# One weight conversion moved into the seam between two batches of attention, and the first query and key loads cut in two

## The chip, the cores and the metric

The kernel runs on one core of a Trainium2 chip. Its time is the device time of one execution in microseconds (us). Five engines work side by side, each through its own list of instructions in order: TensorE (PE, with its weight loads as PEld), VectorE (DVE), ScalarE (ACT), GpSimd (POOL), and SyncE (SP), which here only issues DMA transfers. They wait for each other through semaphores.

## The reference

Three stages follow one another. Sizes: 2 batches of 576 tokens, 8 heads of 64, width 512, inner width 1024, 8 experts.

```python
# windowed causal attention
scores = q @ k.T / sqrt(64);  rel = i - j
scores = where((rel >= 0) & (rel < 128), scores - slope[h] * abs(rel), -1e9)
attn = exp(scores - max(scores));  attn /= sum(attn) + 1e-9
x = (attn @ v) as (1152, 512)
# gated product
x = ((x @ w1) * (x @ w2)) @ w3 @ w_out
# one expert for each token, capacity 288 for each expert
probs = softmax(x @ w_gate);  e = argmax(x @ w_gate)
out[i] = probs[i, e] * (relu(x[i] @ E1[e]) @ E2[e])    # 0 where the expert is full
```

The weights w1, w2, w3 and w_out come as 64-bit floats.

## The kernel before

**Attention.** The work of a batch is cut into 4 pairs of heads, and a pair into 3 groups of query blocks (blocks 0 and 1, blocks 2 and 3, the last half block). So group k runs from 0 to 11 for batch 0 and from 12 to 23 for batch 1. For one group the steps are: `att_qk` (TensorE: scores, L233), `att_max` (DVE: add the bias, take the row extreme, L248), `att_exp` (ACT, L259), `att_norm` (DVE, L277, L278; in batch 1 also the scaling of the probabilities, L287), `att_tr` (TensorE transposes, L301, and copies out of PSUM, L303), `att_pv` (TensorE, L321). When a pair of batch 0 is complete, `att_fin` makes its output x: ACT copies the factors (L349), DVE multiplies (L351), and then x is split into a high part (ACT, L71) and a low part (DVE or POOL, L72).

**Conversions.** A piece of w1 or w2 (128x512 values of 64 bit, staged in one of 4 buffers by a 512 KB DMA, L123) becomes two fp32r tiles wh and wl, high and low part. `convert` gives three steps: `begin` (ACT, L135), `bits` (three DVE operations, L138 to L140), `parts` (wh by ACT at L71, then wl by POOL at L72, then the next DMA of the staging plan). The pieces are w_c_m_kp: column chunk c (0 to 3), matrix m (w1 or w2), half kp of the inner axis. The first four (chunk 0) are converted in groups 2, 5, 8 and 10. The other twelve go by the table `CONVS`, which says how many of them group 12 + i takes.

**Gated product of batch 0 between the groups.** In groups 12 to 23 `fill` puts halves of this product (`ab_half`, twelve matmuls of 288 columns, L376 to L378) between the attention steps, one or two at a time. A half with f = 2 or 3 reads chunk 1 of the weights, one with f = 4 or 5 reads chunk 2. ACT copies the w1 half out of PSUM (asb, L383), DVE multiplies the w2 half with it (g, L388). Two PSUM banks serve the halves in turn.

**The seam.** Group 12 is written out by hand: x of the last pair of batch 0 is finished while TensorE runs the part of two halves that doesn't need it (`part=0`), then the scores of group 13, three zero products (`warm_b`) and the rest of the first half.

**The start.** `keep_clock(12, "warm0")` issues twelve products of zeros (L81) on TensorE; `load_qk(0, 0)` and `load_qk(0, 1)` load the first two pairs: q, k and two pieces of v each. The scores of groups 0, 1 and 2 follow the zero products on TensorE.

The order of the work is the order of the code: the scheduler is off (`manual_schedule`), so each engine runs its instructions as they are written.

```python
CONVS = (0, 1, 1, 2, 1, 1, 2, 1, 1, 1, 1, 0)
        cvts = [c for c in (conv_next() for _ in range(CONVS[k - NGB])) if c]
        for c in cvts: c[0]()
        if k > NGB: fill(ab0, 1); att_tr(k - 1)
        if NGB < k < 2 * NGB - 1: att_qk(k + 1)
        for c in cvts: c[1]()
        if k > NGB: fill(ab0, 2 if k % 3 == 2 else 1)
        for c in cvts: c[2]()
        if k > NGB: att_pv(k - 1)
```

Of the kernel before, what the change touches and what calls it, by code (L numbers as in the profile page):

```python
# [18 lines left out]
P = 128  # L19
# [1 line left out]
BIGS = 31  # L21
STAGES = 4
WARM = (4, 4, 4, 2, 2, 2, 2, 2, 2, 2, 2)
CONVS = (0, 1, 1, 2, 1, 1, 2, 1, 1, 1, 1, 0)
OOB = 1 << 20


# [1 line left out]
def block_kernel(ctx: ExitStack, tc: tile.TileContext, qT, kT, v, w1, w2, w3T, wo, wg, e1, e2, out):  # L29
    nc = tc.nc  # L30
    B, H, D, S = qT.shape
# [26 lines left out]
    def slot(name, shape, dtype=F32R):  # L58
        t = big.tile([P, SLOT], dtype, tag="u", name=name)
        n = 1  # L60
        for d in shape:
            n *= d
        if len(shape) == 1:
            return t[:, :n]
        return t[:, :n].rearrange("p (a b) -> p a b", b=shape[1])

    def ps(tag, name):
        return psum.tile([P, 512], F32, tag=tag, name=name, bufs=2)
# [8 lines left out]
    def keep_clock(n, name):  # L77

        w = ps("t", name)
        for _ in range(n):  # L80
            nc.tensor.matmul(w, hot[:, :P], hot, start=True, stop=True)  # L81

    keep_clock(12, "warm0")


    WC = 256
# [73 lines left out]
    def load_qk(b, hp):  # L160
        h0 = 2 * hp
        t = slot(f"qk_{b}_{hp}", (2, S), F32)
        for i, src in enumerate((qT, kT)):
            nc.sync.dma_start(out=t[:, i, :], in_=src[b, h0 : h0 + 2].rearrange("h d s -> (h d) s"))
        vt = apool.tile([P, 6, P], F32, tag="v", name=f"v_{b}_{hp}", bufs=3)
        cs = slice(h0 * D, (h0 + 2) * D)
        nc.sync.dma_start(out=vt[:, 0:4, :], in_=v[b, 0 : 4 * P, cs].rearrange("(c p) d -> p c d", p=P))
        nc.sync.dma_start(out=vt[:TK, 4:6, :], in_=v[b, S - 2 * TK : S, cs].rearrange("(c p) d -> p c d", p=TK))
        qk[b, hp] = t, vt

    load_qk(0, 0)
    load_qk(0, 1)

    iota = cv.tile([P, 512], F32, tag="cvt", name="iota", bufs=3)[:, : 2 * P]
# [33 lines left out]
    def conv_w(c, m, kp):  # L208
        if kp == 0:
            wsb[m, c] = slot(f"wh{m}_{c}", (KD, WC)), slot(f"wl{m}_{c}", (KD, WC))  # L210
        return convert(("w", c, m, kp), *(w[:, 2 * kp : 2 * kp + 2, :].rearrange("p k f -> p (k f)") for w in wsb[m, c]), pool_hi=(c == 0))
# [12 lines left out]
    def att_qk(k):  # L224
        b, hp, g = groups[k]
        t = qk[b, hp][0]
        tag = "acc" if k <= NGB and k % 2 else "s"
        sps = [ps(tag, f"s{j}_{k}").rearrange("p (i w) -> p i w", i=2) for j in range(2)]
        for gj, i in enumerate(g):
            q0, M, k0, W, _, _ = blocks[i]  # L230
            for j in range(2):
                js = slice(j * D, (j + 1) * D)
                nc.tensor.matmul(sps[j][:M, gj, :W], t[js, 0, q0 : q0 + M], t[js, 1, k0 : k0 + W], start=True, stop=True)  # L233
        live["s", k] = sps

    def att_max(k, gj):
        b, hp, g = groups[k]
        if gj == 0:
            live["p", k] = [], apool.tile([P, 12], F32, tag="sm", name=f"stat_{k}", bufs=8)
        pp, st = live["p", k]  # L240
        i = g[gj]
        q0, M, k0, W, _, _ = blocks[i]
        off = P - (q0 - k0)
        p = apool.tile([P, 2, 2 * P], F32, tag="p", name=f"p_{k}_{i}", bufs=6)
        pp.append(p)
        for j in range(2):
            c = 2 * gj + j
            nc.vector.tensor_tensor_reduce(out=p[:M, j, :W], in0=live["s", k][j][:M, gj, :W],  # L248
                                           in1=relb[:M, 2 * hp + j, off : off + W], scale=-1.0 / isq, scalar=3.0e38,
                                           op0=ALU.add, op1=ALU.min, accum_out=st[:M, c : c + 1])  # L250

    def att_exp(k, gj):
        b, hp, g = groups[k]
        pp, st = live["p", k]
        p = pp[gj]
        _, M, _, W, _, _ = blocks[g[gj]]
        for j in range(2):
            c = 2 * gj + j
            nc.scalar.activation(out=p[:M, j, :W], in_=p[:M, j, :W], func=AF.Exp, scale=-1.0,  # L259
                                 bias=st[:M, c : c + 1], accum_out=st[:M, 4 + c : 5 + c])  # L260
# [97 lines left out]
    def att_fin():  # L358
        if fins:
            fins.pop(0)()  # L360
# [290 lines left out]
    def conv_next():  # L651
        return conv_w(*wq.pop(0)) if wq else None
# [10 lines left out]
    for k in range(NGB):  # L663
        b, hp, g = groups[k]
        if g[0] == 4:
            load_qk(*divmod(hp + 2, NPAIR))
        cvt = conv_next() if k in (2, 5, 8, 10) else None
# [30 lines left out]
    def fill(q, n):  # L698
        for _ in range(n):
            if q:  # L700
                u = q.pop(0)
                ab_half(*u, part=1 if u in begun else None)

    for k in range(NGB, 2 * NGB):
        b, hp, g = groups[k]
        if g[0] == 2 and hp + 2 < NPAIR:
            load_qk(1, hp + 2)
        if k == NGB:

            att_fin()  # L710
            att_norm(k - 1)
            att_tr(k - 1)
            att_pv(k - 2)
            att_pv(k - 1)

            for u in ab0[:2]:
                ab_half(*u, part=0)
            begun = ab0[:2]
            att_max(k, 0)
            att_exp(k, 0)  # L720
            att_fin()
            att_max(k, 1)
            att_exp(k, 1)
            att_fin()
            att_qk(k + 1)
            keep_clock(3, "warm_b")
            fill(ab0, 1)
        elif k == NGB + 1:
            att_soft(k, lambda: (att_norm(k - 1), fill(ab0, 1)))
            att_fin()  # L730
        else:
            att_soft(k, lambda: att_norm(k - 1))
            att_fin()
        cvts = [c for c in (conv_next() for _ in range(CONVS[k - NGB])) if c]
        for c in cvts:
            c[0]()
        if k > NGB:
            fill(ab0, 1)
            att_tr(k - 1)
        if NGB < k < 2 * NGB - 1:  # L740
            att_qk(k + 1)
        for c in cvts:
            c[1]()
        if k > NGB:
            fill(ab0, 2 if k % 3 == 2 else 1)
        for c in cvts:
            c[2]()
        if k > NGB:
            att_pv(k - 1)
# [34 lines left out]
    for i, u in enumerate(ab1):  # L784
# [3 lines left out]
        if i == 2:  # L788
            nc.sync.dma_start(out=disp[0 : E * CAP, :].rearrange("(p r) c -> p r c", p=P),
                              in_=zrow.unsqueeze(1).to_broadcast([P, E * CAP // P, RW]))  # L790
    for at in sorted(jobs):
        for job in jobs[at]:
            job()
    nc.sync.dma_start(out=out.rearrange("(p r) c -> p r c", p=P),
                      in_=zrow[:, :DM].unsqueeze(1).to_broadcast([P, NT // P, DM]))
# [86 lines left out]
    with (tc.If(fullest > N0), tc.tile_pool(name="over", bufs=2) as op,  # L882
          tc.tile_pool(name="overp", bufs=2, space=bass.MemoryType.PSUM) as opp):
        for e in range(E):
# [6 lines left out]
            for r in range(N0, CAP, P):  # L891
                n = min(P, CAP - r)
# [15 lines left out]
                for f in range(EF // P):  # L908
# [4 lines left out]
                    out=out, out_offset=bass.IndirectOffsetOnAxis(ap=x[:n, DM + 1 : DM + 2].bitcast(U32), axis=0),  # L913
                    in_=y[:n], in_offset=None, bounds_check=NT - 1, oob_is_err=False)
# [45 lines left out]
```

## Time and profile before

| what | value |
|---|---|
| time, median of 3 runs | 470.45 us (469.55 to 470.5) |
| the profiled execution: its own time | 469.5 us |
| the profiled execution: span from first to last instruction | 467.8 us |
| TensorE busy | 453.2 us, 97% of the span |
| VectorE, ScalarE, GpSimd busy | 68%, 56%, 31% |
| mean granted TensorE clock | 0.990 of full speed |

The profile is of one execution. 1.7 us of its own time lie outside the span. Matmuls are pipelined and overlap in the records, so a busy TensorE isn't one at its peak; a row in brackets tells how long the engine sat idle before an instruction and what ended the wait. Times in the rows are us from the start of the span. Rows of the timeline that are alike and stand together are merged, with their count behind an x.

### The profile page before, as it was taken

How to read it: one execution, taken by the hardware profiler on the slowest of the kernel's cores; microseconds unless marked ns; L12 is line 12 of the kernel's file. 1: busy time of each engine (PE TensorE's matmuls, PEld its weight loads, DVE VectorE, ACT ScalarE, POOL GpSimd, SP SyncE). 2: the span in 40 equal slices, each digit the busy share in tenths (PEclk: the TensorE clock that was granted, in tenths of full speed). 3: DMA queues.
4: the chain of work that ended last, by engine and by line, in shares of the span. 5: the costliest groups of instructions: out<-in, count | busy, mean ns of one | idle time of the engine just before them, and what ended most of it. 6: DMA issues, size and time to landing. Idle time of an engine off the chain costs nothing.

```text
span 467.8 us, 9288 instructions
## 1 busy us (share of the span) xinstructions
PE 453.2 (97%) x3346; PEld 405.2 (87%) x3346; DVE 320.0 (68%) x860; ACT 261.5 (56%) x653; POOL 144.9 (31%) x154
## 2 busy tenths in 40 slices
PE   8999999989999999999999999989999999999993
PEld 4667887869899999999999999689889898898982
DVE  6786768786542454788756777447888787888840
ACT  5786656465432345434444554246767677676740
POOL 2125113222111132344321111214365454544531
PEclk9999998989999999999999999999999999999998
DMA  8755325322159444585422434284786887868001
GB/s 273 242 183 184 100 74 189 98 84 90 47 170 245 130 136 130 186 303 163 145 89 69 136 136 137 87 296 162 235 291 205 303 243 238 282 206 284 27 1 54
DMA packets 30769, 77.77 MB, mean 166 GB/s; under 512 B 3582, under 2 KB 9214, under 8 KB 30720
## 3 DMA queue, kind: packets, MB, share of 16 engines
q1 hardware_dynamic: 28976, 72.41, 49.6%
q0 software_dynamic: 1744, 4.73, 2.7%
q8 instruction: 28, 0.46, 0.4%
q14 instruction: 21, 0.17, 0.1%
HBM read 65.30 MB, written 12.61 MB: 167 GB/s over the span
## 4 chain that ended last, share of the span: by engine, by line
PE 78%; DVE 10%; issue 6%; ACT 3%; POOL 2%; DVEq 0%; POOLq 0%; ACTq 0%
PE h L581 10%; PE ab L376 7%; PE ab L378 7%; PE ab L377 6%; PE h L582 5%; PE x L474 4%; PE x L475 4%; PE x L476 4%; DVE t_w L140 3%; PE s L233 3%; PE t L301 3%; PE oa L321 3%; PE y L612 3%; PE warm L81 3%; PE y L615 3%
## 5 line engine op out<-in xcount | busy, mean ns | idle before, releaser
L72 DVE TENSOR_TENSOR le<-st_e,he 128x1024 fp32r<-128x1024 f32 x64 | 78.3, 1225 | 28.4 <-ACT he L71 25.1
L376 PE MATMUL ab<-x,wh 128*128 128x288 f32 x256 | 80.3, 314 | 0.8 <-ACT wh L71 0.7
L378 PE MATMUL ab<-x,wl 128*128 128x288 f32 x256 | 76.4, 298 | 1.3 <-POOL wl L72 1.3
L581 PE MATMUL h<-xs,he 128*128 128x384 f32 x256 | 76.6, 357 | 1.1 <-DVE xs L72 1.1
L598 POOL CAST hs<-hs 128x64 fp32r<-128x64 f32 x64 | 53.7, 846 | 76.6 <-ACT hs L594 75.3
L377 PE MATMUL ab<-x,wh 128*128 128x288 f32 x256 | 75.8, 296 | 0.0
L71 ACT CAST he<-st_e 128x1024 fp32r<-128x1024 f32 x64 | 67.2, 1052 | 0.0
L582 PE MATMUL h<-xs,le 128*128 128x192 f32 x256 | 64.1, 251 | 0.0
L376 PEld LDWEIGHTS ab<-x,wh 128*128 128x128 f32 x256 | 48.6, 190 | 6.5 <-issue 2.4
L581 PEld LDWEIGHTS h<-xs,he 128*128 128x128 f32 x256 | 48.0, 188 | 3.8 <-DVE xs L72 1.2
L582 PEld LDWEIGHTS h<-xs,le 128*128 128x128 f32 x256 | 48.7, 190 | 1.9
L378 PEld LDWEIGHTS ab<-x,wl 128*128 128x128 f32 x256 | 48.6, 190 | 2.0 <-POOL wl L72 2.0
L377 PEld LDWEIGHTS ab<-x,wh 128*128 128x128 f32 x256 | 48.7, 190 | 0.0
L388 DVE TENSOR_TENSOR g<-ab,asb 128x288 f32<-128x288 f32 x32 | 14.6, 456 | 48.0 <-PE ab L378 45.8
L259 ACT ACTIVATE p<-p,stat 128x256 f32<-128x256 f32 (+2 forms) x80 | 37.3, 470 | 13.1 <-DVE stat L248 13.1
L588 ACT COPY cr<-h 128x192 f32<-128x192 f32 x64 | 20.5, 320 | 40.2 <-PE h L582 38.3
L474 PE MATMUL x<-wph,gh 128*128 128x260 f32 x144 | 41.4, 287 | 0.0
L476 PE MATMUL x<-wph,gl 128*128 128x260 f32 x144 | 40.6, 282 | 0.0
L475 PE MATMUL x<-wpl,gh 128*128 128x260 f32 x144 | 40.6, 282 | 0.0
L383 ACT COPY asb<-ab 128x288 f32<-128x288 f32 x32 | 12.7, 398 | 47.9 <-PE ab L378 47.9
L440 PE MATMUL wp<-woh,w3h 128*128 128x260 f32 x128 | 36.3, 283 | 0.5 <-DVE wpl L72 0.5
L442 PE MATMUL wp<-woh,w3l 128*128 128x260 f32 x128 | 36.2, 283 | 0.0
(139 smaller groups left out, 1075.1 us busy)
## 6 DMA issues: line engine op xcount, KB each, us to landing
st_e<-e SPq DMA_DIRECT2D x64, 512.0 KB, 4.4
st_w<-w SPq DMA_DIRECT2D x16, 512.0 KB, 4.4
st_w<-w3T SPq DMA_DIRECT2D x16, 512.0 KB, 4.2
disp<-zrow SPq DMA_DIRECT2D x1, 4626.0 KB, 21.3
st_wo<-wo SPq DMA_DIRECT2D x8, 512.0 KB, 3.8
qk<-qT SPq DMA_DIRECT2D x8, 288.0 KB, 4.8
qk<-kT SPq DMA_DIRECT2D x8, 288.0 KB, 5.1
y<-zrow SPq DMA_DIRECT2D x1, 2304.0 KB, 10.7
```

The source lines that it names most:

```text
L71: nc.scalar.copy(out=hi, in_=t)
L72: eng.tensor_tensor(out=lo, in0=t, in1=hi.bitcast(F32), op=ALU.subtract)
L259: nc.scalar.activation(out=p[:M, j, :W], in_=p[:M, j, :W], func=AF.Exp, scale=-1.0, bias=st[:M, c : c + 1], accum_out=st[:M, 4 + c : 5 + c])
L376: nc.tensor.matmul(a[:, :NCH], hi[:, fs], xh[:, n], start=first, stop=False)
L377: nc.tensor.matmul(a[:, :NCH], hi[:, fs], xl[:, n], start=False, stop=False)
L378: nc.tensor.matmul(a[:, :NCH], lo[:, fs], xh[:, n], start=False, stop=last)
L474: nc.tensor.matmul(pa[:, :HG], gh[:, kt, :], th, start=(kt == 0), stop=False)
L475: nc.tensor.matmul(pa[:, :HG], gh[:, kt, :], tl, start=False, stop=False)
L476: nc.tensor.matmul(pa[:, :HG], gl[:, kt, :], th, start=False, stop=(kt == KF - 1))
L581: nc.tensor.matmul(hp_[:, : 2 * N0], hi[:, kt, fs], xs, start=(kt == 0), stop=False)
L582: nc.tensor.matmul(hp_[:, N0 : 2 * N0], lo[:, kt, fs], xs[:, :N0], start=False, stop=(kt == KD - 1))
L598: nc.gpsimd.tensor_copy(h[:, 2 * N0 :], h[:, P:N0])
```

## The change

Three edits.

1. `CONVS` gives group 14 two conversions instead of one, group 15 one instead of two, and group 18 one instead of two. The group of the seam (12) keeps its 0 in the table, but its code now takes one conversion itself: `begin` ahead of the first maxima, `bits` ahead of the first `att_fin` there, `parts` behind the third. So the same sixteen conversions run in the same sequence; those of groups 13 to 17 and the first of group 18, seven in all, now stand one group earlier each (that of group 13 in the seam), and the second of group 18 and all later ones stand where they stood.
2. The zero products at the start are eight instead of twelve.
3. The first load of q and k is done in two column parts: columns 0 to 255 of q, the same of k, then columns 256 to 575 of each. It is four DMAs instead of two ahead of the first v.

```diff
-CONVS = (0, 1, 1, 2, 1, 1, 2, 1, 1, 1, 1, 0)
+CONVS = (0, 1, 2, 1, 1, 1, 1, 1, 1, 1, 1, 0)
-    keep_clock(12, "warm0")
+    keep_clock(8, "warm0")
 def load_qk(b, hp):
-        for i, src in enumerate((qT, kT)):
-            nc.sync.dma_start(out=t[:, i, :], in_=src[b, h0 : h0 + 2].rearrange("h d s -> (h d) s"))
+        for n in (slice(0, 2 * P), slice(2 * P, S)) if b == hp == 0 else (slice(0, S),):
+            for i, src in enumerate((qT, kT)):
+                nc.sync.dma_start(out=t[:, i, n], in_=src[b, h0 : h0 + 2].rearrange("h d s -> (h d) s")[:, n])
...
             begun = ab0[:2]
+            cvt = conv_next()
+            cvt[0]()
             att_max(k, 0)
             att_exp(k, 0)
+            cvt[1]()
             att_fin()
             att_max(k, 1)
             att_exp(k, 1)
             att_fin()
+            cvt[2]()
             att_qk(k + 1)
```

On DVE at the seam, before (x_w and t_w are tiles of a conversion, named w_c_m_kp; rs_3 is the product that makes x of pair 3; a number at a name's end only numbers the tile):

```order
L248 ISA p_12_0_762,stat_12_761<-s0_12_636,relb_117 128x128
L248 ISA stat_12_761 128x1
L248 ISA p_12_0_762,stat_12_761<-s1_12_637,relb_117 128x128
L248 ISA stat_12_761 128x1
L351 TENSOR_TENSOR rs_3_740<-oa_0_3_697,rs_3_740 128x512
L351 TENSOR_TENSOR rs_3_740<-ob_0_265,rs_3_740 128x64
```

and now:

```order
L250 ISA p_12_0_765,stat_12_764<-s0_12_634,relb_115 128x128
L250 ISA stat_12_764 128x1
L250 ISA p_12_0_765,stat_12_764<-s1_12_635,relb_115 128x128
L250 ISA stat_12_764 128x1
L138 TENSOR_SCALAR x_w_1_0_0_762<-st_w_1_0_0_434 128x512
L139 SCALAR_TENSOR_TENSOR x_w_1_0_0_762<-st_w_1_0_0_434,x_w_1_0_0_762 128x512
L140 SCALAR_TENSOR_TENSOR t_w_1_0_0_761<-t_w_1_0_0_761,x_w_1_0_0_762 128x512
L353 TENSOR_TENSOR rs_3_738<-oa_0_3_695,rs_3_738 128x512
L353 TENSOR_TENSOR rs_3_738<-ob_0_263,rs_3_738 128x64
```

The three steps of piece 1_0_0 now stand between the maxima and the product rs_3; on ACT its `begin` stands ahead of the exponentials of group 12 and its wh behind the high part of x.

On DVE at the end of group 15, before (g is the product of two halves, p_16 the maxima of the next group, stat_15 the norm of group 15):

```order
L388 TENSOR_TENSOR g_0_0_814<-ab1_0_1_1_1003,asb_0_1_1_966 128x288
L138 TENSOR_SCALAR x_w_1_1_0_998<-st_w_1_1_0_678 128x512
L139 SCALAR_TENSOR_TENSOR x_w_1_1_0_998<-st_w_1_1_0_678,x_w_1_1_0_998 128x512
L140 SCALAR_TENSOR_TENSOR t_w_1_1_0_997<-t_w_1_1_0_997,x_w_1_1_0_998 128x512
L138 TENSOR_SCALAR x_w_1_1_1_1000<-st_w_1_1_1_876 128x512
L139 SCALAR_TENSOR_TENSOR x_w_1_1_1_1000<-st_w_1_1_1_876,x_w_1_1_1_1000 128x512
L140 SCALAR_TENSOR_TENSOR t_w_1_1_1_999<-t_w_1_1_1_999,x_w_1_1_1_1000 128x512
L248 ISA p_16_2_1073,stat_16_1072<-s0_16_1024,relb_117 128x256
```

and now:

```order
L390 TENSOR_TENSOR g_0_0_824<-ab1_0_1_1_1020,asb_0_1_1_982 128x288
L138 TENSOR_SCALAR x_w_2_0_0_1018<-st_w_2_0_0_884 128x512
L139 SCALAR_TENSOR_TENSOR x_w_2_0_0_1018<-st_w_2_0_0_884,x_w_2_0_0_1018 128x512
L140 SCALAR_TENSOR_TENSOR t_w_2_0_0_1017<-t_w_2_0_0_1017,x_w_2_0_0_1018 128x512
L250 ISA p_16_2_1083,stat_16_1082<-s0_16_1041,relb_115 128x256
```

Both pieces of w2's chunk 1 have left this place for group 14, and the first piece of chunk 2 has come here.

On DVE at the end of group 18, before:

```order
L138 TENSOR_SCALAR x_w_2_1_0_1267<-st_w_2_1_0_1057 128x512
L139 SCALAR_TENSOR_TENSOR x_w_2_1_0_1267<-st_w_2_1_0_1057,x_w_2_1_0_1267 128x512
L140 SCALAR_TENSOR_TENSOR t_w_2_1_0_1266<-t_w_2_1_0_1266,x_w_2_1_0_1267 128x512
L138 TENSOR_SCALAR x_w_2_1_1_1269<-st_w_2_1_1_1147 128x512
L139 SCALAR_TENSOR_TENSOR x_w_2_1_1_1269<-st_w_2_1_1_1147,x_w_2_1_1_1269 128x512
L140 SCALAR_TENSOR_TENSOR t_w_2_1_1_1268<-t_w_2_1_1_1268,x_w_2_1_1_1269 128x512
L388 TENSOR_TENSOR g_0_1_1109<-ab1_0_3_1_1306,asb_0_3_1_1285 128x288
```

and now:

```order
L250 ISA stat_18_1259 128x1
L138 TENSOR_SCALAR x_w_2_1_1_1275<-st_w_2_1_1_1067 128x512
L139 SCALAR_TENSOR_TENSOR x_w_2_1_1_1275<-st_w_2_1_1_1067,x_w_2_1_1_1275 128x512
L140 SCALAR_TENSOR_TENSOR t_w_2_1_1_1274<-t_w_2_1_1_1274,x_w_2_1_1_1275 128x512
L390 TENSOR_TENSOR g_0_1_1117<-ab1_0_3_1_1308,asb_0_3_1_1290 128x288
```

Piece 2_1_0 has left group 18 for group 17. TensorE's own order is unchanged but for the four zero products; on SP, the load of piece 1_1_1 now stands ahead of the loads of q, k and v of batch 1's third pair, and the load of piece 2_1_1 ahead of those of its fourth.

## Rows read from the trace of the kernel before

**Rows 1.** The page's busy line: us (share of the span) xinstructions

```profile
PE 453.2 (97%) x3346; PEld 405.2 (87%) x3346; DVE 320.0 (68%) x860; ACT 261.5 (56%) x653; POOL 144.9 (31%) x154
```

**Rows 2.** PE's waits over the whole span: us in total, times, longest

```profile
PE t L301 <- DVE p L287: 2.0, 1, 2.0
PE ab L378 <- POOL wl L72: 1.3, 3, 0.8
```

**Rows 3.** Timeline of PE around group 15's product: start, us, what

```profile
69.09 0.46 PE L321 MATMUL ob<-pt,v 96*64 96x64 f32 x8
70.22 0.40 PE L376 MATMUL ab<-x,wh 128*128 128x288 f32 x1 [0.67 <-ACT wh L71]
...
71.58 0.40 PE L378 MATMUL ab<-x,wl 128*128 128x288 f32 x1 [0.83 <-POOL wl L72]
...
76.09 0.40 PE L376 MATMUL ab<-x,wh 128*128 128x288 f32 x1
```

**Rows 4.** Timeline of PE around group 18's transposes

```profile
91.56 0.46 PE L321 MATMUL ob<-pt,v 96*64 96x64 f32 x8
91.95 0.40 PE L376 MATMUL ab<-x,wh 128*128 128x288 f32 x1
...
95.78 1.41 PE L301 MATMUL t<-ident,p 128*128 128x128 f32 x6 [1.99 <-DVE p L287]
...
100.57 0.93 PE L321 MATMUL oa<-pt,v 128*64 128x128 f32 x12
```

**Rows 5.** Windows: us, busy PE PEld DVE ACT POOL, PEclk, DMA share, GB/s

```profile
73.00:73.50 0.50, 0.50 (x3) 0.50 (x4) 0.50 (x3) 0.00 (x0) 0.00 (x0) 0.50 1.32 381
97.00:98.00 1.00, 1.00 (x6) 0.34 (x5) 1.00 (x5) 1.00 (x5) 0.00 (x0) 0.50 0.00 0
```

**Rows 6.** Timeline of PE in groups 13 and 14: the same steps undisturbed

```profile
52.43 0.81 PE L301 MATMUL t<-ident,p 128*128 128x128 f32 x6
53.65 0.40 PE L376 MATMUL ab<-x,wh 128*128 128x288 f32 x1
...
55.44 0.93 PE L321 MATMUL oa<-pt,v 128*64 128x128 f32 x12
```

**Rows 7.** Timeline of the start: zero products, first scores, first conversion

```profile
1.25 4.22 PE L81 MATMUL warm<-hot 128*128 128x512 bf16 x12 [1.25 <-DVE hot L75]
...
4.21 0.77 PEld L81 LDWEIGHTS <-hot 128*128 128x128 bf16 x4 [0.28 <-issue]
...
5.41 2.75 PE L233 MATMUL s<-qk 64*128 64x128 f32 x20
...
11.58 0.68 ACT L135 ACTIVATE t_w<-st_w 128x512 f32<-128x512 f32 x1
```

**Rows 8.** DMAs issued at 1.0 to 1.5 and 4.6 to 5.0: us to landing

```profile
qk<-kT SPq DMA_DIRECT2D x1, 288.0 KB, 3.3
...
st_w<-w SPq DMA_DIRECT2D x1, 512.0 KB, 6.3
```

**Rows 9.** Timeline of the seam: the waits of DVE and ACT, POOL's work

```profile
42.63 1.41 POOL L72 TENSOR_TENSOR x<-rs,x 128x576 fp32r<-128x576 f32 x1 [0.16 <-ACT x L71]
...
45.28 0.59 ACT L349 COPY rs<-ra 128x512 f32<-128x512 f32 x1 [1.04 <-PE ra L344]
...
45.90 0.69 DVE L351 TENSOR_TENSOR rs<-oa,rs 128x512 f32<-128x512 f32 x1 [2.71 <-ACT rs L349]
...
50.27 0.40 ACT L383 COPY asb<-ab 128x288 f32<-128x288 f32 x1 [1.52 <-PE ab L378]
```

**Rows 10.** Lines L138 and L140 on DVE: duration ns min/median/max

```profile
L138 DVE TENSOR_SCALAR x_w<-st_w x32: 411/419/1461, 13.4 to 233.3; 128x512 int32<-128x512 int32 x32
L140 DVE SCALAR_TENSOR_TENSOR t_w<-t_w,x_w x32: 691/693/1625, 14.6 to 234.6; 128x512 int32<-128x512 int32 x32
```

**Rows 11.** Timeline around 70: POOL's two low parts, DVE's scaling

```profile
70.25 2.53 POOL L72 TENSOR_TENSOR wl<-t_w,wh 128x512 fp32r<-128x512 f32 x2 [4.62 <-ACT wh L71]
...
71.81 1.78 DVE L287 TENSOR_SCALAR p<-p,stat 128x128 f32<-128x128 f32 x4
```

## The prediction

> **What bounds the kernel now.** I read the page's busy line first. TensorE is busy 97% of the span and no other engine over 68% [rows 1], so time is to be had where TensorE stands still or runs slowly, and anything done on VectorE, ScalarE or GpSimd is free as long as TensorE doesn't wait for it. The second view is the list of TensorE's waits over the whole span. It is short, and two of its entries point at the conversions: 2.0 us once at a transpose that waits for VectorE's scaling of the probabilities, and 1.3 us in three waits for a low part of the weights from GpSimd [rows 2]. The third view is TensorE's timeline at these places.
>
> The first place is the w2 half of the product with f = 2, the first reader of w2's chunk 1. TensorE is done with `att_pv` of group 14 and waits 0.67 for the high part of piece 1_1_0, then 0.83 for its low part [rows 3]. Both pieces of that chunk are converted in group 15, just ahead of the reader. The second place is the transposes of group 18: the scaling comes 1.99 us late [rows 4], because two conversions stand ahead of it on VectorE.
>
> The fourth view, the windows, shows what a wait costs beyond itself. Behind both places the granted clock is 0.50 [rows 5], the lower of its two levels (1.2 GHz instead of 2.4), and the same instructions take about twice as long. TensorE had stood still for most of 2 us before each fall.
>
> **The first place.** From the start of `att_pv` to the second next product, TensorE takes 76.09 - 69.09 = 7.00 [rows 3]. The same steps undisturbed: `att_pv` of the half block 91.95 - 91.56 = 0.39 [rows 4], twelve products 55.44 - 53.65 = 1.79, transposes and scores 53.65 - 52.43 = 1.22 [rows 6], together 3.40. The wait and the slow clock behind it cost 3.60.
>
> The change converts these two pieces in group 14. Their reader then comes a whole group later, which is several us, while GpSimd's two low parts take 2.53 [rows 11]. So both waits go.
>
> **The second place.** From the twelve products to the next `att_pv` it is 100.57 - 91.95 = 8.62 [rows 4]. Undisturbed it is 1.79 + 1.22 + 1.79 = 4.80 [rows 6]. That costs 3.82. Of the two conversions of group 18 one moves to group 17. One conversion takes 0.42 + 0.69 + 0.69 = 1.80 on VectorE (L139 is like L140) [rows 10], almost all of the 1.99; and one of the two low parts leaves as well.
>
> What is late next? VectorE and GpSimd hold each other up. While GpSimd made two low parts, four scalings on VectorE took 1.78 [rows 11]; L138 takes 0.42 as a rule but up to 1.46, and L140 0.69 but up to 1.63 [rows 10]. So a scaling that meets a low part is up to about a GpSimd operation late. Half of the 2.53 for two is 1.27 for one. With the conversions one group earlier, the low parts fall at other moments of the groups, and the scaling ahead of the transposes of groups 13, 15 and 16 can meet one. I can't read from a trace of the old order how they fall. Each such meeting costs TensorE between nothing and 1.27. I take half, 0.6, at three places: +1.8 (ends 0 and +3.8).
>
> **The seam.** One conversion is added to group 12. VectorE idles for 2.71 ahead of the product of the last pair, from 43.19 to 45.90 [rows 9]. GpSimd's low part of x runs from 42.63 to 44.04 [rows 9], so L138, which can be held up by it, is taken to wait for its end. Then 44.04 + 1.80 = 45.84: just in time. Behind it are queued the product that makes x and two maxima, and TensorE waits for that x. There is 0.06 left, so I put +0.1 (ends: 0, and 1.8 if nothing is hidden).
>
> ScalarE gets `begin` (0.68 for the like instruction [rows 7]) ahead of the exponentials; it idles for 1.04 before the copy of the factors [rows 9]. The high part of the weight goes behind that of x and ahead of the copy of the first half, where it idles for 1.52 [rows 9]. Both are hidden, and the cover stays since TensorE sets the times of both copies.
>
> On SP the load of piece 1_1_1 now stands ahead of those of batch 1's third pair. The pair is needed four groups later, so I put nothing (to lose would be a wait of TensorE at its scores, which the trace doesn't show today).
>
> Group 14 now has two conversions, 3.60 on VectorE, ahead of a product of two halves that frees a PSUM bank. Group 15 had the same load before, in the same place of its code, and the waits there were for the weights, not for a bank [rows 3]. I put it into the +1.8.
>
> **The start.** Four zero products go. Their weight loads are (0.77 - 0.15)/3 = 0.21 apart [rows 7], the last 0.15 being one load's length, so four are 0.84. The first scores start at 5.41, when the products end at 1.25 + 4.22 = 5.47 [rows 7]. k has landed by 4.3 to 4.8 (issued between 1.0 and 1.5, 3.3 to land) [rows 8]. So today the products decide, and with eight, the scores could start at about 4.57, near the time at which a whole k lands. The first column parts are less than half the bytes and are all that group 0 reads, so the cut takes the loads out of the way there.
>
> Not all of the 0.84 will last. The first conversion's `begin` on ScalarE is at 11.58 [rows 7], and its weights land between 10.9 and 11.3 (issued between 4.6 and 5.0, 6.3 to land) [rows 8]. Moved up by 0.84 it would be at 10.74 and wait 0.2 to 0.6, with the copies of the transposes queued behind it on ScalarE. I take -0.6 for the start. Ends: -0.84; and, if a transfer of half the size took as long as a whole one, the loads behind would be late by up to the 3.3 of one [rows 8], so 3.3 - 0.84 = +2.5. The bytes are the same, so I stay near the first.
>
> The Trainium skill (DMA: Bandwidth & Descriptors, section on measured bandwidth) speaks against the cut: a small transfer reaches a smaller share of the rate, 0.95 us for 64 KB and 6.15 us for 1 MB. Drawing a line between the two, as an estimate, two parts of 128 KB and two of 160 KB take 5.5 us one behind the other, where two of 288 KB take 4.3; by that all later loads are 1.2 late and the sum is 0.8 to 1.2 smaller. No row here shows a 128 KB load by itself.
>
> **The sum.** -3.60 - 3.82 + 1.8 + 0.1 - 0.6 = -6.1. The profiled execution's own time is 469.5 (span 467.8 and 1.7 around it), so it becomes 463.4. The median of the runs is 470.45, 0.95 above the profiled execution. The forecast for the median is 470.45 - 6.1 = 464.3. Behind group 19 the order is unchanged, and no entry of TensorE's waits names a DMA [rows 2], so the gain should reach the end.
>
> **Rivals.**
>
> *The loads come late.* The mechanism is the one above: the four parts push the queue back and ScalarE's first conversion waits. For it: its weights have only 0.3 to 0.7 to spare. Against it: the same bytes. The start then gives about +0.3 instead of -0.6: 465.2.
>
> *One fall of the clock stays.* The meetings of scaling and low part add up to near 2 us at one place, as before both falls, and TensorE falls to the low clock again. For it: the 1.78 and the maxima of 1.46 and 1.63 [rows 10, 11]. Against it: fewer conversions at one place. One of the two gains goes, about 3.7, while the others hold: 468.0.
>
> *VectorE becomes the bound of groups 12 to 17: slower.* Seven conversions move one group earlier. If their 1.80 on VectorE lands on the way to a transpose or to x, each costs TensorE its full length. The gains without any new wait are 3.60 + 3.82 + 0.84 = 8.26, so it decides from 8.26/1.80 = 4.6, that is from five of seven. With six, 10.8 - 8.3 = +2.5: 473.0. For it: in the seam just 0.06 is left, and a late x delays everything. Against it: VectorE is busy 68% only [rows 1], and the same work was hidden one group later at all but two places.
>
> *Nothing comes of it.* A later stage takes the time back, as it waits for transfers: 470.5. Against it: no such wait in [rows 2].
>
> *All goes well.* No new wait: 470.45 - 8.26 = 462.2.
>
> **Chances.** Forecast 0.56, late loads 0.12, one fall stays 0.14, slower 0.08, nothing 0.05, all well 0.05. What can be told from no change is 0.2%, 0.94 us. So faster: 0.87; within 0.2%: 0.05; slower: 0.08. The range for 8 in 10 goes from 461.8, just below the case without new waits, to 468.5, which takes in the rival with one fall and leaves out no change and slower.
>
> **What would show it.** Right: no wait for a weight part at the w2 half of f = 2, and none of 1 us or more at group 18's transposes; granted clock 1.00 from the first scores through batch 1's groups; first scores at 4.5 to 4.7; the rs product at the seam no more than 0.2 later, counted from the end of the factor matmuls. Wrong: a new wait of TensorE for VectorE's scaling at groups 13 to 16 of 1 us or more, a low clock behind it, or the seam's product with x standing until VectorE or ScalarE is done with the conversion. A first `begin` on ScalarE that waits for a DMA speaks for the late loads.

## The result, and the profile after

The changed kernel takes 464.3 us (median of 5 runs, 463.89 to 464.79) against 469.55 for the kernel before, run beside it (469.05 to 470.5). The ratio is 0.9884, 95% interval 0.9871 to 0.9896. The time is the forecast to a tenth, but the change is a little smaller than it: 5.45 us (4.9 to 6.1, from the ratio) where 6.1 were forecast, counted from the 470.45 of the first three runs of the kernel before. The agreement to a tenth is luck in part: the same 6.1 taken off the 469.55 of the runs beside it would have given 463.4, and terms of the sum were off in opposite directions, as the experiments show. The profiled execution has a span of 462.6 instead of 467.8.

The page's busy line of the changed kernel, which answers to [rows 1] (lines of the new code are two higher: the products are L378 to L380, the transposes L303, the scaling L289):

```profile
PE 451.1 (98%) x3342; PEld 403.3 (87%) x3342; DVE 321.7 (70%) x860; ACT 261.8 (57%) x653; POOL 144.7 (31%) x154
```

TensorE's waits of the changed kernel over the whole span, which answer to [rows 2]: us in total, times, longest.

```profile
PE t L303 <- DVE p L289: 0.6, 2, 0.4
...
PE ab L380 <- POOL wl L72: 0.3, 1, 0.3
```

The wait of 2.0 at the transposes is gone, of the three for a low part one of 0.3 is left, and two short waits for the scaling stand in the list that the list before doesn't have.

The timeline of TensorE in the changed kernel: the product of group 15 and the group behind it, then group 18 and the group behind it. It answers to [rows 3, 4].

```profile
69.32 0.46 PE L323 MATMUL ob<-pt,v 96*64 96x64 f32 x8
...
71.40 1.06 PE L303 MATMUL t<-ident,p 128*128 128x128 f32 x6
...
73.17 0.41 PE L378 MATMUL ab<-x,wh 128*128 128x288 f32 x1
...
75.83 0.40 PE L378 MATMUL ab<-x,wh 128*128 128x288 f32 x1
...
77.94 1.15 PE L303 MATMUL t<-ident,p 128*128 128x128 f32 x8 [0.24 <-DVE p L289]
...
79.88 0.40 PE L378 MATMUL ab<-x,wh 128*128 128x288 f32 x1
...
89.55 0.40 PE L378 MATMUL ab<-x,wh 128*128 128x288 f32 x1
...
91.24 1.09 PE L303 MATMUL t<-ident,p 128*128 128x128 f32 x6
...
93.02 0.40 PE L378 MATMUL ab<-x,wh 128*128 128x288 f32 x1
...
94.80 0.44 PE L323 MATMUL oa<-pt,v 128*64 128x128 f32 x4
...
97.87 1.15 PE L303 MATMUL t<-ident,p 128*128 128x128 f32 x8 [0.35 <-DVE p L289]
...
99.81 0.40 PE L378 MATMUL ab<-x,wh 128*128 128x288 f32 x1
```

The first place takes 73.17 - 69.32 = 3.85 where it took 7.00 [rows 3], the second 94.80 - 89.55 = 5.25 where it took 8.62 [rows 4]: -3.15 and -3.37. Undisturbed they would take 3.40 and 4.80 [rows 3, 4, 6], so 0.45 of delay is left in each. In the first there are waits of the weight loads, which the list of TensorE's matmul waits doesn't hold. The timeline of PEld there:

```profile
72.02 0.20 PEld L303 LDWEIGHTS t<-ident,p 128*128 128x128 f32 x2 [0.26 <-DVE p L289]
72.39 0.50 PEld L235 LDWEIGHTS s<-qk 64*64 64x64 f32 x4 [0.17 <-DVE stat L250]
73.17 0.19 PEld L378 LDWEIGHTS ab<-x,wh 128*128 128x128 f32 x1 [0.28 <-ACT p L261]
```

The windows behind both places, which answer to [rows 5], show no fall of the granted clock (PEclk, the number behind POOL's); it falls nowhere else before the last microseconds of the span:

```profile
72.00:75.00 3.00, 2.98 (x21) 2.24 (x20) 2.86 (x10) 2.40 (x7) 0.00 (x0) 1.00 0.81 223
95.00:99.00 4.00, 3.65 (x34) 3.00 (x30) 3.90 (x14) 3.03 (x8) 1.28 (x1) 1.00 0.46 131
```

In groups 13, 16 and 19 the stretch from one product to the second next is longer than in the profile before. Rows of the timeline before around the transposes of groups 13, 16 and 19:

```profile
56.30 0.40 PE L376 MATMUL ab<-x,wh 128*128 128x288 f32 x1
...
59.80 0.40 PE L376 MATMUL ab<-x,wh 128*128 128x288 f32 x1
...
78.75 0.40 PE L376 MATMUL ab<-x,wh 128*128 128x288 f32 x1
...
82.28 0.40 PE L376 MATMUL ab<-x,wh 128*128 128x288 f32 x1
...
101.42 0.40 PE L376 MATMUL ab<-x,wh 128*128 128x288 f32 x1
...
104.94 0.40 PE L376 MATMUL ab<-x,wh 128*128 128x288 f32 x1
```

Group 16 takes 79.88 - 75.83 = 4.05 against 82.28 - 78.75 = 3.53: +0.52. Group 13 gives 3.71 - 3.50 = +0.21, from the rows here and the first two of these of the changed kernel:

```profile
56.32 0.40 PE L378 MATMUL ab<-x,wh 128*128 128x288 f32 x1
...
60.03 0.40 PE L378 MATMUL ab<-x,wh 128*128 128x288 f32 x1
...
95.65 0.40 PE L378 MATMUL ab<-x,wh 128*128 128x288 f32 x1
```

Group 19 gives +0.64 in the same way (99.81 - 95.65 = 4.16 against 104.94 - 101.42 = 3.52). From the end of group 13's stretch to the first place both profiles take 9.29 (69.32 - 60.03, before 69.09 - 59.80), so the two conversions of group 14 add nothing there. Together -3.15 - 3.37 + 0.21 + 0.52 + 0.64 = -5.15, all of the -5.2 of the spans. By these two profiles, then, the start gave nothing. The rows of the changed kernel's start, TensorE, VectorE and ScalarE, which answer to [rows 7]:

```profile
1.26 3.59 PE L81 MATMUL warm<-hot 128*128 128x512 bf16 x8 [1.26 <-DVE hot L75]
4.78 3.41 PE L235 MATMUL s<-qk 64*128 64x128 f32 x20
...
6.39 0.29 DVE L250 CUSTOM_DVE_ANT_0 p<-s,relb 128x128 f32<-128x128 f32 x1 [2.15 <-PE s L235]
...
12.44 0.66 ACT L135 ACTIVATE t_w<-st_w 128x512 f32<-128x512 f32 x1 [0.74 <-DMA st_w<-w]
```

The scores start 0.63 earlier than before (4.78, where the prediction's sign of being right was 4.5 to 4.7), but the same 20 of them take 3.41 instead of 2.75, and VectorE gets its first one at 6.39 where it had it at 6.37. The loads came late, as one rival said: ScalarE's first conversion waits 0.74 for them.

In the seam L138 is held by GpSimd's low part of x, which ends at 42.66 + 1.41 = 44.07, as forecast. VectorE's timeline there, which answers to [rows 9]:

```profile
43.14 1.22 DVE L138 TENSOR_SCALAR x_w<-st_w 128x512 int32<-128x512 int32 x1
...
45.92 0.69 DVE L353 TENSOR_TENSOR rs<-oa,rs 128x512 f32<-128x512 f32 x1
```

The product of the last pair starts at 45.92 instead of 45.90: the seam is full to the last 0.1 us and costs 0.02.

### The profile page after: what moved, and what is told of

Read it like the earlier page. It is cut to its first block, busy times and chain, and to the rows that moved or that the text cites. A ratio compares the mean times of both kernels' runs of the same rounds, so it can differ in the third digit from the quotient of the medians.

```text
span 462.6 us, 9290 instructions
## 1 busy us (share of the span) xinstructions
PE 451.1 (98%) x3342; PEld 403.3 (87%) x3342; DVE 321.7 (70%) x860; ACT 261.8 (57%) x653; POOL 144.7 (31%) x154
## 3 DMA queue, kind: packets, MB, share of 16 engines
q0 software_dynamic: 1744, 4.73, 2.8%
## 4 chain that ended last, share of the span: by engine, by line
PE 77%; DVE 12%; issue 6%; ACT 2%; POOL 1%; DVEq 0%; POOLq 0%; ACTq 0%
PE h L583 11%; PE ab L378 7%; PE ab L380 6%; PE ab L379 6%; PE h L584 5%; PE x L476 4%; PE x L477 4%; PE x L478 4%; DVE t_w L140 4%; PE s L235 3%; PE t L303 3%; PE y L614 3%; PE oa L323 3%; PE y L617 3%; PE y L615 3%
## 5 line engine op out<-in xcount | busy, mean ns | idle before, releaser
L378 PE MATMUL ab<-x,wh 128*128 128x288 f32 x256 | 79.7, 311 | 0.1
L380 PE MATMUL ab<-x,wl 128*128 128x288 f32 x256 | 75.5, 295 | 0.3 <-POOL wl L72 0.3
L378 PEld LDWEIGHTS ab<-x,wh 128*128 128x128 f32 x256 | 48.0, 188 | 5.3 <-issue 2.2
L380 PEld LDWEIGHTS ab<-x,wl 128*128 128x128 f32 x256 | 48.0, 188 | 0.6 <-POOL wl L72 0.6
L379 PEld LDWEIGHTS ab<-x,wh 128*128 128x128 f32 x256 | 48.1, 188 | 0.0
```

Source lines behind the costliest of these rows:

```text
L378: nc.tensor.matmul(a[:, :NCH], hi[:, fs], xh[:, n], start=first, stop=False)
L379: nc.tensor.matmul(a[:, :NCH], hi[:, fs], xl[:, n], start=False, stop=False)
L380: nc.tensor.matmul(a[:, :NCH], lo[:, fs], xh[:, n], start=False, stop=last)
```

## The experiments

My theory after the two profiles was that the conversions carry all of the gain and the start nothing. The first four kernels each have one part of the change alone.

**Conversions and seam alone.** The changed kernel with `keep_clock(12, "warm0")` and whole loads:

```
-    keep_clock(8, "warm0")
+    keep_clock(12, "warm0")
...
-        for n in (slice(0, 2 * P), slice(2 * P, S)) if b == hp == 0 else (slice(0, S),):
+        for n in (slice(0, S),):
```

> The changed kernel with its start undone: twelve zero products, q and k of the first pair in whole loads; the conversions and the seam as in the change. Theory (the conversions carry everything, the start is worth nothing): all of the 5.2 us, a ratio of 0.9885 to the kernel before, within 0.001; ScalarE's first conversion starts near 11.6 without waiting for a load. Rival (the start was worth the forecast 0.6 us and the new waits were larger than they look): 0.6 us less, a ratio of 0.990.

Measured: 465.16, ratio 0.9903 (0.989 to 0.9916). That is the rival's number. The theory's 0.9885 lies just outside the interval, the upper end of its band inside it.

**The start alone**, on the kernel before (CONVS and seam as there):

```
-    keep_clock(12, "warm0")
+    keep_clock(8, "warm0")
```

and the cut of the loads as in the change.

> The kernel before with the start of the change alone: eight zero products and the first pair's q and k in two column parts; conversions as before. Theory: no difference, a ratio of 1.000 within 0.001; scores begin near 4.8 but run at the lower clock until about 6.2, the first maximum on VectorE stays near 6.4, and ScalarE's first conversion waits about 0.7 us for its weights. Rival: the first maximum comes 0.6 us earlier and the ratio is 0.9987.

Measured: 468.54, ratio 0.9974 (0.9965 to 0.9983). My theory falls: the start is worth 1.2 us (0.8 to 1.6), more than the rival's 0.6 too. Of the theory's two signs in the trace one is there (the first maximum is at 6.46), the other not (ScalarE's first conversion has no wait). Its two halves apart, eight products with whole loads (the edit above alone):

> The kernel before with eight zero products instead of twelve, q and k in whole loads. If the cut into parts is what makes ScalarE's first conversion wait for its weights, that wait isn't here and the conversion starts near 11.6. What the first scores wait for here is open: the whole k lands at 4.3 to 4.8 in the profile before, so they should begin near 4.8 either way. If the clock rises at a fixed time after the first product whatever their number (4.25 before), the scores run at full clock from the start and the first maximum on VectorE comes 0.6 us early, ratio 0.9987; if it rises at about 6.2 when fewer products run, the first maximum stays near 6.4, ratio 1.000.

and the cut with twelve products:

> The kernel before with the first pair's q and k in two column parts, twelve zero products. Theory: the first scores start at 5.4 at full clock as before, the first maximum near 6.4; ScalarE's first conversion waits for its weights, which land about 0.9 us later than before (12.4 instead of 11.6), and this is hidden before TensorE: ratio 1.000 within 0.001. Rival: the later weights push everything behind them by 0.9 us, ratio 1.0019.

Measured: eight products alone 0.9977 (0.9966 to 0.9988), the cut alone 1.0005 (0.9996 to 1.0015). So the products carry the start, and the cut does nothing that can be measured in time. The wait of ScalarE's first conversion was missed: with the cut and twelve products it starts at 12.63 without one, since the scores ahead of it were late too.

Why did the two profiles show nothing? Start rows of three kernels. Conversions alone, twelve products:

```profile
1.25 5.06 PE L81 MATMUL warm<-hot 128*128 128x512 bf16 x12 [1.25 <-DVE hot L75]
6.25 2.75 PE L235 MATMUL s<-qk 64*128 64x128 f32 x20
...
7.20 0.29 DVE L250 CUSTOM_DVE_ANT_0 p<-s,relb 128x128 f32<-128x128 f32 x1 [2.88 <-PE s L235]
```

and two weight loads of its zero products:

```profile
5.07 0.15 PEld L81 LDWEIGHTS <-hot 128*128 128x128 bf16 x1 [0.28 <-issue]
5.50 0.15 PEld L81 LDWEIGHTS <-hot 128*128 128x128 bf16 x1 [0.28 <-issue]
```

Eight products alone:

```profile
1.25 3.44 PE L81 MATMUL warm<-hot 128*128 128x512 bf16 x8 [1.25 <-DVE hot L75]
4.71 2.72 PE L233 MATMUL s<-qk 64*128 64x128 f32 x20
...
5.64 0.29 DVE L248 CUSTOM_DVE_ANT_0 p<-s,relb 128x128 f32<-128x128 f32 x1 [1.39 <-PE s L233]
```

The same twelve products take 4.22 in the profile before [rows 7] and 5.06 here; the same 20 scores take 2.72 to 2.75 or 3.41. The kernel before and the one with the conversions alone have the same instructions up to there, but the weight loads of its products still stand 0.43 apart at 5.07 and 5.50, where those of the profile before stand 0.21 apart from 4.21 on [rows 7]. I read this as TensorE going over from the lower level of its clock (1.2 GHz) to the upper at another moment in another execution. It is worked out from the lengths of equal instructions alone: the clock column reads 1.00 in this stretch of every profile. Compared like with like, the first maximum comes at 6.39 with eight products and 7.20 with twelve where the rise is late, at 5.64 and 6.37 where it is early: 0.81 and 0.73 earlier. My reading of the start had compared an early rise (before) with a late one (after).

The same profile of eight products alone shows something else. It has the conversions of the kernel before and all its waits. Its timeline of TensorE at the same places:

```profile
68.36 0.46 PE L321 MATMUL ob<-pt,v 96*64 96x64 f32 x8
69.50 0.40 PE L376 MATMUL ab<-x,wh 128*128 128x288 f32 x1 [0.67 <-ACT wh L71]
...
74.06 0.40 PE L376 MATMUL ab<-x,wh 128*128 128x288 f32 x1
...
78.82 0.41 PE L301 MATMUL t<-ident,p 128*128 128x128 f32 x2 [0.25 <-DVE p L287]
...
90.42 0.40 PE L376 MATMUL ab<-x,wh 128*128 128x288 f32 x1
...
94.28 1.09 PE L301 MATMUL t<-ident,p 128*128 128x128 f32 x6 [2.01 <-DVE p L287]
...
97.84 0.33 PE L321 MATMUL oa<-pt,v 128*64 128x128 f32 x2
...
100.91 0.30 PE L301 MATMUL t<-ident,p 128*128 128x128 f32 x1 [0.36 <-DVE p L287]
```

and its windows behind the two places (PEclk is the number behind POOL's):

```profile
72.00:74.00 2.00, 1.90 (x14) 1.52 (x14) 2.00 (x9) 0.77 (x3) 0.05 (x1) 1.00 1.07 345
95.00:98.00 3.00, 3.00 (x23) 2.28 (x23) 2.86 (x9) 2.69 (x8) 0.00 (x0) 1.00 0.00 0
```

The waits are those of [rows 3, 4], but no fall of the clock follows either of them. The first place takes 74.06 - 68.36 = 5.70, the second 97.84 - 90.42 = 7.42, so a fall costs 1.30 and 1.20 there. And groups 16 and 19 have the waits of 0.25 and 0.36 that I took for new ones of the change. They belong to the old order too, and so do the whole delays: its stretches there take 80.75 - 76.70 = 4.05 and 102.85 - 98.69 = 4.16, as in the change. In the profile before, TensorE at its low clock came later to them. The delay at group 18 is older as well: from the first transposes to the second next product this run takes 96.06 - 94.28 = 1.78 behind the wait, and the change 93.02 - 91.24 = 1.78, against 1.22 undisturbed [rows 6]. So a fall nets 1.30 - 0.52 = 0.78 and 1.20 - 0.64 = 0.56, and the conversions are worth 5.15 against an execution with both falls and 5.15 - 1.34 = 3.81 against one with none. Of the 28 executions of the kernel before that were timed beside these four, 15 have a mean granted clock of 0.989 or 0.990, as the profiled one with its two falls, and 13 of 0.996, as the two profiles without one (the start alone has one fall, behind the second place, and 0.993). If that is how they divide, the mean gain is (15 x 5.15 + 13 x 3.81) / 28 = 4.53; the conversions alone measured 0.0097 x 469.49 = 4.55.

The agreement proves less than it seems to. In the run with eight products the two groups stand apart as the net price says: 469.19 is the mean of its six executions at 0.989 or 0.990, 467.71 that of its five at 0.996 or 0.997, 1.48 between them. But the 15 and the 13 of the kernel before average 469.99 and 469.29, just 0.69 apart, where two falls net 1.34. What can make up the rest is the start: the run with the cut and twelve products has no fall (0.996) but the late rise, and its span of 467.5 is only 0.3 below that of the profile with both falls and the early rise. Whether the 13 rose late, no trace shows. One pair of profiles is alike in both: this run and the conversions alone have the late rise and no fall, and their spans are 467.5 - 463.4 = 4.1 apart, near the 3.81.

**One place at a time.** First the second place alone, on the kernel before:

```
-CONVS = (0, 1, 1, 2, 1, 1, 2, 1, 1, 1, 1, 0)
+CONVS = (0, 1, 1, 2, 1, 2, 1, 1, 1, 1, 1, 0)
```

> The kernel before with one number of its table changed twice: group 18 gives one of its two conversions to group 17; start, seam and groups 12 to 16 as before. Theory (the granted clock falls behind a wait in some executions and not in others, so a fall counts with about half its price): the 2.0 us wait goes and about half of the 1.8 us that the fall cost, 2.6 us, a ratio of 0.9945. Rival (a fall follows every such wait, the price taken in the prediction): 3.82 less one new small wait, 3.2 us, 0.9932.

Then the first place alone, with the seam of the change:

```
-CONVS = (0, 1, 1, 2, 1, 1, 2, 1, 1, 1, 1, 0)
+CONVS = (0, 1, 2, 0, 1, 1, 2, 1, 1, 1, 1, 0)
```

> The kernel before with only the two pieces of w2's chunk 1 converted in group 14 (one conversion moves into the seam, group 15 has none); group 18 keeps its two conversions; start as before. Theory (half price of a fall): the 1.5 us of waits go, new waits of 0.3 to 0.6 come, about 1.0 us of slow clock goes: 1.9 us, ratio 0.996; with the run that repairs group 18 alone this adds up to the 4.55 us of all conversions moved. Rival (full price): 3.60 less 1.2 of new waits, 2.4 us, 0.9949; and a third, that the two places only pay together, since a repaired first place brings the fall to the second: 1.0 us or less, 0.998.

Measured: 467.62, ratio 0.9946 (0.9932 to 0.9961), nearest to the theory of half a price, with the rival's 0.9932 at the end of the interval, and 466.34, ratio 0.9922 (0.9905 to 0.9939), which is more than any of the three said: 3.7 us. The two add up to 6.2, more than the 4.55 of all conversions moved. Part of the excess can lie in the base: of the 15 executions of the kernel before that were timed beside these, 12 have a mean clock of 0.990 or 0.991, against 15 of 28 beside the first four, and their median is 469.96 instead of 469.49. The first place of this kernel, from `att_pv` at 69.40 to the second next product at 72.70, shows another part. It takes 3.30, none of the 0.45 that the change leaves there, and its group 16 has no wait: group 15 has no conversion here and one in the change. Its second place still waits 2.0, and in this execution the clock falls behind it.

**The table without the seam.** On the kernel before:

```
-CONVS = (0, 1, 1, 2, 1, 1, 2, 1, 1, 1, 1, 0)
+CONVS = (0, 2, 2, 1, 1, 1, 1, 1, 1, 1, 1, 0)
```

> The conversions of the change without its seam: group 13 does two conversions, group 12 none; start as before. If the seam is what makes it pay, group 13's scaling comes late behind 3.6 us of VectorE's conversion work as group 18's did, 2.0 us and in some executions a fall of the clock: ratio 0.994 to 0.997. Rival: VectorE has room in group 13 too and the seam is only another place for the same work: 0.990, as with all conversions moved.

Measured: 465.86, ratio 0.991 (0.9892 to 0.9928). Against 0.9903 with the seam nothing can be told in time, so the rival holds there. The trace does show a price of leaving the seam out, a wait at group 13's transposes, short of the 2.0 that I expected:

```profile
59.26 1.15 PE L301 MATMUL t<-ident,p 128*128 128x128 f32 x8 [1.11 <-DVE p L287]
```

**Who holds the scaling?** The changed kernel with the low parts of w1 and w2 made on VectorE:

```
-                split(t, dst_hi, dst_lo, nc.gpsimd)
+                split(t, dst_hi, dst_lo, nc.vector if u[0] == "w" else nc.gpsimd)
```

> The changed kernel with the low part of w1 and w2 computed on VectorE instead of GpSimd. Theory (a scaling that meets GpSimd's low part is held until that ends, and this makes the 0.24 and 0.35 us waits of two transposes): the scalings of groups 13, 15 and 16 take their 0.5 to 0.8 again instead of 1.2, 2.04 and 2.10, but VectorE has 0.6 more per conversion; the waits stay at 0.3 or less in all or are gone, the 0.3 us wait for a low part goes, and the time stays within 0.5 us of the changed kernel: ratio to the kernel before 0.988 within 0.001. Rival (the scalings are long because of their own order on VectorE, not because of GpSimd): they stay at 2 us, and with 0.6 more per conversion the waits grow to 1 us or more: 0.991 or above.

The 40 scalings in the changed kernel, duration ns min/median/max:

```profile
L289 DVE TENSOR_SCALAR p<-p,stat x40: 280/344/1443, 51.0 to 122.7; 128x256 f32<-128x256 f32 x24, 128x128 f32<-128x128 f32 x8, 64x192 f32<-64x192 f32 x8
```

and in this one, with VectorE's low parts from the view by line (busy us, mean ns, idle before):

```profile
L289 DVE TENSOR_SCALAR p<-p,stat x40: 279/346/357, 51.3 to 129.4; 128x256 f32<-128x256 f32 x24, 128x128 f32<-128x128 f32 x8, 64x192 f32<-64x192 f32 x8
...
L72 DVE TENSOR_TENSOR wl<-t_w,wh 128x512 fp32r<-128x512 f32 x12 | 8.2, 689 | 9.0 <-ACT wh L71 9.0
```

The mechanism is shown: without a low part on GpSimd no scaling takes over 0.36, with it up to 1.44. The time was missed by both sides: 471.2, ratio 1.0022 (1.0013 to 1.0032). VectorE now stands 9.0 us in front of the 12 low parts until ScalarE has made the high part, with the scaling queued behind, and the transposes wait 4.6 in seven waits.

**Fewer products, and no cut.** The changed kernel with `keep_clock(4, "warm0")`:

> The changed kernel with four zero products in front instead of eight. If the products still decide when the scores start, 0.8 us more is gained: ratio to the kernel before about 0.9865 against 0.988 for the change. If the first parts of q and k decide (they land at about 3.5 to 4.0) the scores start near 4.0 and no more than 0.5 us comes. If fewer products let the clock rise later, the first scores run at half speed for longer and nothing comes: 0.988.

and with whole loads (`for n in (slice(0, S),)`):

> The change without the cut of the first pair's q and k: conversions, seam and eight products as in the change, whole loads. Theory (the cut is worth nothing and its later loads are hidden): as the changed kernel, ratio 0.988 within 0.0015. Rival (the cut is needed for the scores to start at 4.8 with eight products): 0.8 us slower, 0.990.

Measured: 464.34, ratio 0.9895 (0.9881 to 0.9909), and 464.38, ratio 0.9886 (0.9871 to 0.99). Neither differs from the change. With four products the load decides, as the second reading said, and then the second pair's k is late too: TensorE waits 0.47 for k at its first scores, which start at 3.62, and 0.48 at those of 9.45. The third reading has a row as well: the 20 scores take 3.60.

**Two better tables?** The changed kernel with group 15 emptied as in the first-place run, and the conversion given to group 17:

```
-CONVS = (0, 1, 2, 1, 1, 1, 1, 1, 1, 1, 1, 0)
+CONVS = (0, 1, 2, 0, 1, 2, 1, 1, 1, 1, 1, 0)
```

> The changed kernel with two moves more in its table: group 15 gives its conversion to group 17 (0, 1, 2, 0, 1, 2, ...). Theory (the new waits of the change are 0.55 at group 15 and 0.51 at group 16, both behind group 15's conversion; in the run with group 15 empty both are gone): 1.0 us less than the change, ratio to the kernel before 0.986. Rival (two conversions in group 17 hold up group 18's transposes, as two in group 15 held up group 16's maxima): the gain is given back there, 0.988.

and with group 18's conversion in group 17 as well:

```
-CONVS = (0, 1, 2, 1, 1, 1, 1, 1, 1, 1, 1, 0)
+CONVS = (0, 1, 2, 0, 1, 3, 0, 1, 1, 1, 1, 0)
```

> As the run before, and group 18's conversion also goes to group 17 (three there, none in 18). Theory (a group behind a half group is free of waits when it has no conversion): the wait of group 19's transposes, 0.35 and about 0.65 with its neighbours, goes too: 1.6 us less than the change, ratio 0.985. Rival (three conversions, 5.4 us of VectorE in one half group, are too many): a wait of 1 us or more at group 18's transposes, 0.989 or above.

Measured: 463.77, ratio 0.9873 (0.9859 to 0.9887), the fastest of all, though its interval overlaps that of the change, and 467.88, ratio 0.9954 (0.9938 to 0.997). In the first, the first place takes 3.29 and group 16 has no wait, as the theory said, but three products on, the stretch from one product to the second next takes 5.79 instead of 5.24 (88.83 - 83.04, in the changed kernel 89.55 - 84.31), so half of the gain is given back.

The same profile holds a wait that bears on the cut. Its 20 first scores take 2.85, nearer to the early rise, and then TensorE waits for k of the second pair:

```profile
9.81 0.93 PE L235 MATMUL s<-qk 64*128 64x128 f32 x8 [0.43 <-DMA qk<-kT]
```

With eight products alone, whole loads and the early rise, the same scores had no wait:

```profile
9.11 0.93 PE L233 MATMUL s<-qk 64*128 64x128 f32 x8
```

In the kernel before they start at 9.83. So in this execution the later loads of the cut took back nearly all that the eight products had gained up to these scores.

In the second table the rival is right, with TensorE's longest wait of all:

```profile
87.51 0.45 PE L303 MATMUL t<-ident,p 64*96 64x64 f32 x4 [2.36 <-DVE p L289]
```

## Why the prediction was right, and where it was not

**First and second place** (-3.60 and -3.82): both waits went, as argued. The sizes held for the profile on which they rest: -3.15 and -3.37, and with the delay of 0.45 that stays in each, 3.60 and 3.82. They were too large for the median of the runs. The step behind that is "Behind both places the granted clock is 0.50", taken as if a fall followed each such wait; the run with eight products and the one with the cut have the same waits without one. In time all conversions gave -4.55 (-5.2 to -3.9) where the terms with +1.8 and +0.1 make -5.5. How much of the difference is the missing falls is not shown, since the executions that were not profiled divide as they do only by inference.

**New waits** (+1.8 at three places): 0.45, 0.45, 0.21, 0.52 and 0.64, together 2.27, in the profile of the change against the undisturbed steps, 0.5 more than the term. The mechanism, scaling held by GpSimd's low part, is shown by the run with the low part on VectorE. Two of the places were not named, groups 18 and 19, and the delays at groups 16, 18 and 19 stand in the old order too, so only 0.45 + 0.21 at the first place and group 13 is new. The two conversions of group 14 cost nothing up to the first place (9.29 in both profiles); what costs there is the one left in group 15, since both runs without it take 3.30 and 3.29.

**Seam** (+0.1): 0.02 on VectorE, as worked out to the instruction.

**Start** (-0.6): the 0.84 was cut to -0.6 for loads that would come late, and the path of that loss was wrong. They did come late. The cut puts two more issues on SP, and the first weight load is issued at 5.68 instead of 4.73; k of the second pair lands at 4.18 + 5.5 = 9.68 instead of 3.23 + 5.1 = 8.33. In the change the first conversion on ScalarE waits 0.74 for it; of the seven profiles with the cut five have such a wait (0.27 to 1.46), of the seven without it none. But TensorE's list has no wait that follows from that one. What it does wait for, in the one profile with eight products, the cut and the early rise, is k of the second pair (0.43), which the prediction did not name. In the profile of the change, with the late rise, these scores start at 9.86, behind the landing of k, and nothing was lost. The start was worth 0.73 and 0.81 in the profiles compared alike and 1.2 (0.8 to 1.6) in time. By the Trainium skill's page DMA: Bandwidth & Descriptors (section on measured bandwidth) I had estimated later loads of 1.2; a delay of that size is there (1.35 for k of the second pair), and 0.95 of it is the later issue, of which that section says nothing. The smaller gain that I worked out from it isn't there in time; in the traces it shows only in that one profile.

So in time the conversions gave about 1.0 less than their terms and the start 0.2 to 1.0 more than its own.

**Rivals.** The loads that come late were real, hidden in the profile of the change and not in that of the first better table. No fall of the clock stayed in the profile of the change. VectorE as the bound is what the runs with three conversions in one group and with the low part on VectorE show; two in group 14 did not reach it.

**Open.** What decides, in one execution and not in another, whether the clock falls behind the same wait, and how many executions rise early. That the executions of the kernel before at 0.990 are those with two falls is inferred from their mean clocks, and the 0.69 between the two groups fits it only together with a difference in the start; one execution of the kernel before was profiled.

## What to carry to other kernels

A fall of the clock in one profile is a price that some executions pay and others don't: take a wait at its own length first, and what the fall adds as a share. Before two profiles are compared at their start, look at the length of equal instructions to see whether the clock had risen. Where a stretch of TensorE is long and no wait is listed, look at the waits of its weight loads. And work moved off a crowded place leaves small delays: here 2.3 of the 7.4 stayed. Only 0.7 of it was new; the rest stood in the old order, and one trace of that order, with the low clock at these places, did not show it.

## What was not expected of the hardware

The moment at which the clock first rises differs between two executions with the same start by enough to stretch twelve 128x512 products from 4.22 to 5.06. A wait of 1.99 to 2.01 at the same transposes was followed by the lower clock (0.50) in the profile before and by 1.00 in the run with eight products. With the same loads of q and k, TensorE waited 0.43 for k of the second pair in an execution whose clock rose early and not at all in one where it rose late. A VectorE scaling of 0.28 to 0.36 took up to 1.44 while GpSimd subtracted 128x512 elements, which takes 1.27 to 1.45 itself.
